# Second product with tokens as weights and w_out moving, leftover tokens of two batches in one sum

## Chip, core and metric

One NeuronCore of one Trainium2 chip runs one program. The metric is the device time of one execution in microseconds (us); the time before is the median of three runs. TensorE (PE) multiplies, VectorE (DVE), ScalarE (ACT) and GpSimd (POOL) do the rest, SyncE (SP) issues the transfers.

## What is computed

```python
a = softmax(phi, axis=seq)                  # [8, 8 heads, 576, 32 slots]
k_m = einsum('bhsm,bhsd->bhmd', a, k)       # d = 64
v_m = einsum('bhsm,bhsd->bhmd', a, v)
attn = softmax(q @ k_m.T / 8)               # [8, 8, 576, 32]
x = (attn @ v_m) as [8 * 576, 512]
h = x @ w_in                                # [4608, 2048]
out = gelu(h) @ w_out                       # [4608, 512]
```

All inputs are float32 but the two weights, which arrive as float64 bits and are converted on the chip (softmax sums carry a small 1e-9, left out here).

## The kernel before

The attention output enters only the first product, so that is taken as attn @ U with U = v_m @ w_in: its contraction runs over 8 heads x 32 slots = 256 rows of one batch (two groups g of 128 partitions) in place of 512. Both large products split their operands into two parts of 12 significant bits (float32r; `_hi` and `_lo`, or `gh` and `gl`) and take high x high, high x low and low x high.

A batch has 576 tokens, worked in two halves of 288. The hidden features come in 16 chunks f of 128. One step is (batch, half, f):

- `hidden` (L544): 6 matmuls with U as weights and the half's attention `p_hi`/`p_lo` moving, 288 wide, into one PSUM tile `h` (two of them in turn).
- `gelu` on ACT (L557) to `gf`, then on DVE the cast `gh` (helper, L126) and the difference `gl` (L563).
- `project` (L580): 12 matmuls, 4 blocks of 128 output features times three products, with w_out (`wo_hi`, `wo_lo`) as weights and `gh`/`gl` moving, 288 wide, into the four sums `acc`. The output therefore comes out transposed, features on the partitions.
- `evict` at a half's end (L598 to L604): DVE and ACT copy the four sums in turn to tiles `o`, four buffers, and SP sends each to `outT`.

`project` follows `hidden` two steps behind (LAG = 2). The first batch is cut in segments of f that alternate between the halves, with partial sums in `part`, while the weights are still being converted (`wi_y`, `wo_y`, `wi_raw`, `wo_raw` and the split `wo_lo`, L158 to L189); its order is a string, START, and every engine takes its part of it as it stands there. Behind it the tile framework's scheduler orders each engine. Around the steps goes a plan: `put(t, ...)` gives each piece of the next batch's attention and of its U a step, and no piece may stand more than AHEAD = 4 steps early.

The attention of a batch: exps of phi (L226, and L282 with tokens on partitions), slot products `pk` (L291), transposes `ptk` (L316), scores `psc` (L350), the softmax on DVE and ACT (exp L385), `p_hi`/`p_lo`. ACT loads a table at each change between exp and gelu. U of batch 1 is made by `absorb` (L482, copies L489/L490); from batch 2 on a pair of batches shares `absorb2`: three matmuls 512 wide (L463), an ACT cast (L467), a DVE difference (L468), and an ACT copy of the second batch's half to `uf` (L469), which `u_split` divides later. U has nine tiles in turn; two make up a block of 512 hidden features. `pk`, `ptk`, `psc` and `pu` all take turns in two PSUM tiles (`at`).

Of the kernel before, what the change touches and what calls it, by code (L numbers as in the profile page):

```python
# [39 lines left out]
gh.6 gl.6 dD.o.6 dD.i.7 dB.o.7 Uh.5 Ul.5 Uh.4 gl.7 dE.6 Lwi.13 p.5 p.6 Ul.4 anorm.1  # L40
# [12 lines left out]
def slot_attention_gelu_ffn(  # L53
    ctx: ExitStack,
    tc: tile.TileContext,
    phiT: bass.AP,  # [B, 2, 128 (4 heads, m), S]
    phiN: bass.AP,  # [B, S, 256 (heads, m)]
    qT: bass.AP,  # [B, 4, 128 (2 heads, d), S]
    kv: bass.AP,  # [B, 2, S, 4 heads, (k | v) 128]
    w_in: bass.AP,  # [512, 2048], float64 bits in int64  # L60
    w_out: bass.AP,  # [2048, 512], float64 bits in int64
    outT: bass.AP,  # [512, B * S]
):
# [25 lines left out]
    W_MAX = 8053061632.0  # the float32 with bits 0x4FEFFFFF  # L89
# [150 lines left out]
    def a_T(b, g, c0):  # L240
        """a of 4 heads with positions on the partitions, from chunk c0 on."""
        aT = tile_of(
            ("aT", b), lambda: sb.tile([P, NC, G, P], F32, tag="aT", name=f"aT_{b}", bufs=1)
        )
        cs = range(c0, min(c0 + 4, NC))
        pool, tag = (ps_acc, f"acc{2 * g + c0 // 4}") if b == 0 else (ps_at, "at")
        pt = pool.tile([P, 4, P], F32, tag=tag, name=f"pt_{b}_{g}_{c0}")
        for n, c in enumerate(cs):
            rows = min(P, S - c * P)
            nc.tensor.transpose(  # L250
                pt[:rows, n, :], st["phi", b][:, g, c * P : c * P + rows], ident
            )
        rows = min(P, S - cs[-1] * P)
        copy("a", aT[:rows, c0 : cs[-1] + 1, g], pt[:rows, : len(cs)])
# [29 lines left out]
    def slots(b, g):  # L284
        """k_m and v_m of 4 heads, [(head, m), (k d | v d)], but the sums of a."""
# [25 lines left out]
    def slots_T(b):  # L311
        """Block-diagonal transposes of k_m and v_m: [(2 heads, d), g, (2 pairs, 2 heads, m)]."""
# [164 lines left out]
    def absorb(b, i, g):  # L477
        """U = v_m @ w_in for 4 heads and 512 of the hidden features, split."""
# [13 lines left out]
    def u0_p(f):  # L492
        """The same for the first batch, all heads and 128 hidden features."""
# [33 lines left out]
    for t, x in enumerate(steps):  # L527
        due.setdefault(x[2], t)
    steps += [
        (b, hf, f, f == 0, f == NF - 1, False)  # L530
        for b in range(1, B)
        for hf in range(2)
        for f in range(NF)
    ]
# [24 lines left out]
    def gelu_hi(t):  # L559
        copy("d", g_tile(t, "gh"), st["gf", t])  # L560

    def gelu_lo(t):
        eng("d").tensor_tensor(  # L563
            g_tile(t, "gl"), st["gf", t], st["gh", t].bitcast(F32), op=ALU.subtract
        )

    def project(t):
        """Adds hidden features f to the half's output."""
# [7 lines left out]
        gh, gl = st["gh", t], st["gl", t]  # L576
# [11 lines left out]
    def evict(t):  # L588
        b, hf, f, first, last, more = steps[t]
        col = b * S + hf * HS  # L590
        for d in range(ND):
# [3 lines left out]
            else:  # L595
                o = sb.tile([P, HS], F32, tag="o", name=f"o_{b}_{hf}_{d}", bufs=4)
# [20 lines left out]
        "h": hidden, "gelu": gelu, "gh": gelu_hi, "gl": gelu_lo, "p": project, "o": evict,  # L617
    }
# [30 lines left out]

    AHEAD = 4  # L650
    n = 2 * NF
    # From batch 2 on, the slots of two batches are made before the first one's U.
    begin = {1: 2, 2: n - 10, 3: n + 3}
    for b in range(1, B):
# [43 lines left out]

    LAG = 2
    for t in range(len(steps) + LAG):  # L700
        if t < len(steps):
            for x in (f"h.{t}", f"gelu.{t}", f"gh.{t}", f"gl.{t}"):
                if x not in done:
                    do(x)
# [3 lines left out]
        if k >= 0:
            if f"p.{k}" not in done:
                do(f"p.{k}")  # L710
            if steps[k][4] and f"o.{k}" not in done:
                do(f"o.{k}")
# [35 lines left out]
```

## Time and profile before

| | us |
|---|---|
| median of 3 runs | 780.12 (779.45 to 780.64) |
| profiled execution, first to last instruction (span) | 777.9 |

The time of a run holds the span and 2.2 us around it, taking the median for the profiled execution's own time. Mean granted TensorE clock: 0.973. A row of a timeline has the start in us, the duration, the engine, the line, the operation and the tiles (out<-in), and in brackets the idle time ahead and what ended it. Rows of groups have the count behind an x, then the summed busy time in us, the mean in ns, and the idle time ahead of them with its releasers. The duration of a matmul is modelled and overlaps the next one; for throughput read the distance of two starts. A window's row has its length, and for each engine the busy time and the count, then the granted clock and the share of the transfers.

### The profile page before, as it was taken

The page shows a single profiled execution, that of the slowest core. Times are in us where ns is not written, and L with a number is a line of the kernel's source. Part 1 is how long each engine was busy: PE and PEld are TensorE (multiplying, and loading weights), DVE is VectorE, ACT ScalarE, POOL GpSimd, SP SyncE. Part 2 cuts the span into 40 slices and gives each one's busy share as a digit, 9 for nine tenths or more (in the row PEclk, how much of TensorE's full clock was granted, in tenths as well). Part 3 has the DMA queues.
Part 4 walks back from the last instruction along what each step waited for, and adds up shares of the span by engine and source line. Part 5 has one row for each costly group of instructions (what it writes and reads, how often), then busy time and mean ns, then how long its engine had stood idle before and what let it go on. Part 6 is the DMA issues. An engine that isn't in the chain of part 4 may idle for free.

```text
span 777.9 us, 14426 instructions
## 1 busy us (share of the span) xinstructions
PE 740.3 (95%) x5772; PEld 693.1 (89%) x5772; DVE 509.9 (66%) x1133; ACT 355.7 (46%) x653; POOL 64.5 (8%) x59
## 2 busy tenths in 40 slices
PE   6487889999999999999999999999999999999998
PEld 4276777879999999999999999999999999999997
DVE  3999999756489645766479655756469654755332
ACT  3757567544256435355146435446147532323211
POOL 1566532100000000000000000000000000000000
PEclk8678999999999999999999999999999999999999
DMA  9856552043220140151220040061120010100000
GB/s 287 300 157 210 170 207 86 4 150 123 62 62 1 40 145 31 35 187 55 62 62 1 31 153 32 5 210 62 62 61 2 31 32 25 39 22 10 14 18 32
DMA packets 44932, 63.72 MB, mean 82 GB/s; under 512 B 3520, under 2 KB 31552, under 8 KB 44864
## 3 DMA queue, kind: packets, MB, share of 16 engines
q1 hardware_dynamic: 44864, 62.80, 25.0%
q8 instruction: 45, 0.74, 0.4%
q14 instruction: 23, 0.19, 0.1%
HBM read 53.35 MB, written 9.44 MB: 81 GB/s over the span
## 4 chain that ended last, share of the span: by engine, by line
PE 87%; DVE 7%; issue 2%; DMA 1%; POOL 1%; ACT 1%; SPq 1%; DVEq 0%; POOLq 0%
PE acc L580 50%; PE h L544 25%; PE pu L463 4%; PE pk L291 3%; PE psc L350 2%; DMA kv<-kv 1%; PE pu L482 1%; DVE gl L563 1%; POOL w_in_sb L176 1%; DVE wo_raw L166 1%; DVE wi_raw L166 1%; DVE wo_y L165 1%; DVE wo_y L169 1%; POOL wo_y L183 1%; PE pu L501 1%
## 5 line engine op out<-in xcount | busy, mean ns | idle before, releaser
L580 PE MATMUL acc<-gh,wo_hi 128*128 128x288 f32 x1024 | 309.1, 302 | 3.8 <-DVE part L602 3.8
L580 PE MATMUL acc<-gl,wo_hi 128*128 128x288 f32 x1024 | 303.4, 296 | 3.1 <-DVE gl L563 2.8
L580 PE MATMUL acc<-gh,wo_lo 128*128 128x288 f32 x1024 | 305.2, 298 | 0.0
L557 ACT ACTIVATE gf<-h 128x288 f32<-128x288 f32 x256 | 104.8, 411 | 306.5 <-PE h L544 259.7
L544 PE MATMUL h<-p_hi,U 128*128 128x288 f32 x1024 | 221.5, 298 | 10.0 <-DVE U L516 7.1
L580 PEld LDWEIGHTS acc<-gh,wo_hi 128*128 128x128 f32 x1024 | 194.3, 190 | 20.6 <-issue 9.3
L126 DVE CAST gh<-gf 128x288 fp32r<-128x288 f32 x250 | 77.7, 311 | 200.8 <-ACT gf L557 200.5
L580 PEld LDWEIGHTS acc<-gl,wo_hi 128*128 128x128 f32 x1024 | 194.6, 190 | 4.3 <-DVE gl L563 3.4
L580 PEld LDWEIGHTS acc<-gh,wo_lo 128*128 128x128 f32 x1024 | 194.8, 190 | 3.1 <-issue 1.0
L544 PEld LDWEIGHTS h<-p_hi,U 128*128 128x128 f32 x1024 | 167.1, 192 | 13.1 <-DVE U L516 8.6
L563 DVE TENSOR_TENSOR gl<-gf,gh 128x288 fp32r<-128x288 f32 x254 | 121.8, 482 | 13.2 <-ACT gh L126 0.3
L544 PE MATMUL h<-p_lo,U 128*128 128x288 f32 x512 | 111.9, 301 | 1.2 <-DVE p_lo L423 1.2
L544 PEld LDWEIGHTS h<-p_lo,U 128*128 128x128 f32 x512 | 83.3, 191 | 1.5 <-DVE p_lo L423 1.5
L469 ACT COPY uf<-pu 64x512 f32<-64x512 f32 x48 | 27.9, 581 | 42.0 <-DVE U L468 41.9
L557 ACT ACT_TABLE_LOAD x31 | 39.8, 1283 | 1.7 <-PE h L544 0.9
L467 ACT CAST U<-pu 64x512 fp32r<-64x512 f32 x48 | 27.9, 582 | 13.2 <-PE pu L463 13.0
L468 DVE TENSOR_TENSOR U<-pu,U 64x512 fp32r<-64x512 f32 x48 | 33.0, 688 | 1.4
L436 DVE TENSOR_TENSOR wl<-w_in_sb,wh 128x512 fp32r<-128x512 f32 x48 | 32.8, 684 | 0.7
L176 POOL TENSOR_TENSOR w_in_sb<-wi_y,wi_raw 128x512 int32<-128x512 int32 x16 | 25.7, 1609 | 46.4 <-DVE wi_y L169 29.4
L291 PE MATMUL pk<-kv,aT 128*32 128x128 f32 (+1 forms) x640 | 24.9, 292 | 3.6 <-DMA kv<-kv 2.6
L291 PEld LDWEIGHTS pk<-kv,aT 128*32 128x32 f32 (+1 forms) x640 | 16.6, 114 | 10.5 <-issue 5.3
L183 POOL TENSOR_TENSOR wo_y<-wo_y,wo_raw 128x512 int32<-128x512 int32 x16 | 23.9, 1492 | 22.7 <-DVE wo_y L169 11.6
(95 smaller groups left out, 645.3 us busy)
## 6 DMA issues: line engine op xcount, KB each, us to landing
kv<-kv SPq DMA_DIRECT2D x64, 256.0 KB, 4.4
q<-qT SPq DMA_DIRECT2D x16, 576.0 KB, 4.1
outT<-o SPq DMA_DIRECT2D x64, 144.0 KB, 1.8
wi_raw<-w_in SPq DMA_DIRECT2D x16, 512.0 KB, 5.7
wo_raw<-w_out SPq DMA_DIRECT2D x16, 512.0 KB, 7.0
phi<-phiT SPq DMA_DIRECT2D x16, 288.0 KB, 4.8
aT<-phiN SPq DMA_DIRECT2D x6, 512.0 KB, 5.5
kv<-kv SPq DMA_DIRECT2D x16, 128.0 KB, 4.6
```

Source lines behind the costliest of these rows:

```text
L126: return e.copy(dst, src) if e is nc.scalar else e.tensor_copy(dst, src)
L176: nc.gpsimd.tensor_tensor(w_in_sb[:, :, f * P : (f + 1) * P].bitcast(I32), y.bitcast(I32).rearrange(parts, c=ND), low.rearrange(parts, c=N ...
L183: nc.gpsimd.tensor_tensor(y.bitcast(I32), y.bitcast(I32), low, op=ALU.add)
L291: nc.tensor.matmul(pk[32 * j : 32 * j + 32, :P], st["aT", b][:rows, c, g, 32 * j : 32 * j + 32], t[:rows, j, :], start=(c == 0), stop=(c = ...
L436: nc.vector.tensor_tensor(w_lo, w, w_hi.bitcast(F32), op=ALU.subtract)
L463: nc.tensor.matmul(pu, v.rearrange("p a n -> p (a n)"), w, start=(k == 0), stop=(k == 2))
L467: nc.scalar.copy(u[own, 0, :], pu[own])
L468: nc.vector.tensor_sub(u[own, 1, :], pu[own], u[own, 0, :].bitcast(F32))
L544: i = nc.tensor.matmul(h[:, :HS], u[g][w], x[:, g, :], start=(n == 0), stop=(n == 3 * G - 1))
L557: nc.scalar.activation(g_tile(t, "gf"), st["h", t][:, :HS], AF.Gelu)
L563: eng("d").tensor_tensor(g_tile(t, "gl"), st["gf", t], st["gh", t].bitcast(F32), op=ALU.subtract)
L580: nc.tensor.matmul(acc[d][:, :HS], w[:, f, ds_], x, start=(first and n == 0), stop=(last and n == 2),)
```

## The change

Batches 1 to 7 (all but the first; counting from 1, from batch 2 on) swap the second product's operands: `gh` and `gl` of 128 tokens are the weights and a row block of w_out, 512 features wide, moves. A batch's 576 tokens are four blocks of 128 and 64 left over. So both halves of a chunk are worked in succession (f is now the outer loop, the half the inner one), the gelus of both fill one tile of 512 columns and a tail of 64, and cast and difference run on 512 columns at once. The 64-column tails of all 16 chunks are kept, and those of two batches (2 and 3, 4 and 5, 6 and 7) go through the second product together behind the odd batch; batch 1 has no partner. The output has tokens on its partitions; the first batch keeps its transposed form (`out0T`).

To have both halves' attention ready at a batch's start, and to make room, other things move: attention of both halves and U are planned at other steps; `o` has two buffers instead of four, `gl` and `kT` two instead of three; `vT` uses the tiles of `uf`; `p_hi`/`p_lo` take three turns, one of which (V) occupies U tiles; two more U tiles hold the tails, so five are left in turn for U. In START one piece moves (gl.7 behind p.5).

```diff
-    for t in range(len(steps) + LAG):  # h, gelu, gh, gl of t; plan; p of t - LAG
...
+    behind = [f"p.{n - 1}", f"o.{n - 1}"]
+    for b in range(1, B):
+        for f in range(NF):
+            t = n * b + 2 * f
+            for hf in range(2):
+                dos(f"H.{b}.{f}.{hf}", f"G.{b}.{f}.{hf}")
+                first[t + hf] = st["hi", b, f, hf]
+                if hf:
+                    dos(f"Gh.{b}.{f}", f"Gl.{b}.{f}")
+                run(t + hf)
+            dos(*behind)
+            behind = [f"P.{b}.{f}"]
+        behind += [f"O.{b}.{j}" for j in range(NT)]
+        if b % 2:
+            for k in range(NFB):
+                dos(f"Tg.{b}.{k}")
+                dos(*behind)
+                behind = [f"T.{b}.{k}"]
+            behind += [f"To.{b}"]
+    dos(*behind)
...
+    def gelu_n(b, f, hf):
+        h, gf = st["h", b, f, hf], g_of("gf", b, f)
+        if hf == 0:
+            nc.scalar.activation(gf[:, :HS], h[:, :HS], AF.Gelu)
+        else:
+            nc.scalar.activation(gf[:, HS:], h[:, : MAIN - HS], AF.Gelu)
+            nc.scalar.activation(tail(b, f)[:, b % 2], h[:, MAIN - HS : HS], AF.Gelu)
...
+    def products(acc, f, gh, gl):
+        for n, (x, w) in enumerate(((gh, wo_hi), (gh, wo_lo), (gl, wo_hi))):
+            nc.tensor.matmul(
+                acc, x, w[:, f, :], start=(f == 0 and n == 0), stop=(f == NF - 1 and n == 2)
+            )
+
+    def project_n(b, f):
...
+        for j in range(NT):
+            js = slice(j * P, (j + 1) * P)
+            products(st["acc", b][j], f, gh[:, js], gl[:, js])
+
+    def tail_project(b, k):
...
+        r = slice(TL * (b % 2), TL * (b % 2) + TL) if alone(b) else slice(0, P)
+        for n in range(4):
+            js = slice(n * P + r.start, n * P + r.stop)
+            products(st["tacc", b][: r.stop - r.start], 4 * k + n, gh[:, js], gl[:, js])
+
+    def evict_n(b, j):
+        o = sb.tile([P, DM], F32, tag="o", name=f"o_{b}_{j}", bufs=NO)
+        copy("da"[j % 2], o, st["acc", b][j])
+        r = b * S + j * P
+        nc.sync.dma_start(out[r : r + P, :], o)
+
+    def tail_evict(b):
+        o = sb.tile([P, DM], F32, tag="o", name=f"to_{b}", bufs=NO)
+        bs = (b,) if alone(b) else (b - 1, b)
+        copy("a", o[: TL * len(bs)], st["tacc", b][: TL * len(bs)])
+        for x, c in enumerate(bs):
+            r = c * S + MAIN
+            nc.sync.dma_start(out[r : r + TL, :], o[TL * x : TL * x + TL])
...
-        attend(b, 0, t + 21)
+        attend(b, 0, t + (17 if b > 1 else 22))
+        put(t + (19 if b > 1 else 23), f"Lq.{b}.1")
+        attend(b, 1, t + 26)
...
-                    put(t + 18 + 4 * i + 4 * g, f"U.{b}.{i}.{g}")
+                    put(t + 26.5 + 8 * i + 2 * g, f"U.{b}.{i}.{g}")
...
-                    put(t + 18 + 4 * i + c - 2, f"W.{b}.{i}.{c}")
-                    put(t + 18 + 4 * i + c, f"U2.{b}.{i}.{c}")
+                    put(t + 20 + 8 * i + 2 * c, f"W.{b}.{i}.{c}")
+                    put(t + 22 + 8 * i + 2 * c, f"U2.{b}.{i}.{c}")
-        put(t + n, f"Lq.{b}.1")
-        attend(b, 1, t + n + 3)
```

**DVE towards the end of the first batch's weights.** Rows in order of DVE's queue, before; the `U` row is the difference that the first product's chunk 11 waits for, the row behind it the second batch's first U.

```order
L126 CAST gh_1177<-gf_1175 128x288
L165 TENSOR_SCALAR wi_y<-wi_y 128x512
L563 TENSOR_TENSOR gl_1179<-gf_1175,gh_1177 128x288
L189 TENSOR_TENSOR wo_lo<-wo_y,wo_hi 128x512
L516 TENSOR_TENSOR U_10_1148<-pu_11_1197,U_10_1148 128x2x128
L490 TENSOR_TENSOR U_0_0_1204<-pu_0_0_1205,U_0_0_1204 128x512
L189 TENSOR_TENSOR wo_lo<-wo_y,wo_hi 128x512
```

The same place of DVE's queue after the change:

```order
L139 CAST gh_1177<-gf_1175 128x288
L182 TENSOR_SCALAR wo_y<-wo_y 128x512
L202 TENSOR_TENSOR wo_lo<-wo_y,wo_hi 128x512
L542 TENSOR_TENSOR U_10_1148<-pu_11_1197,U_10_1148 128x2x128
L589 TENSOR_TENSOR gl_1179<-gf_1175,gh_1177 128x288
L202 TENSOR_TENSOR wo_lo<-wo_y,wo_hi 128x512
L178 TENSOR_SCALAR wi_y<-wi_y 128x512
```

The U difference of chunk 11 now stands ahead of this `gl` and of the step `wi_y`, and the second batch's U (L490) has gone from here; with it, on PE, the product `pu_0_0` (L482) that stood behind `pu_11`.

**ACT in the middle of batch 2, before.** Casts `U` and copies `uf` belong to `absorb2` of a pair; `gf` rows are gelus, the table load and `sT` an exp of the scores.

```order
L467 CAST U_0_1_2522<-pu_0_3_2568 64x512
L469 COPY uf_0_2445<-pu_0_3_2568 64x512
L557 ACTIVATE gf_2598<-h_1_6_2591 128x288
L467 CAST U_1_0_2613<-pu_1_0_2615 64x512
L385 ACT_TABLE_LOAD
L385 ACTIVATE sT_0_2562<-sT_0_2562 128x576
L469 COPY uf_1_2614<-pu_1_0_2615 64x512
L557 ACT_TABLE_LOAD
L557 ACTIVATE gf_2645<-h_1_7_2638 128x288
```

After the change, ACT around chunks 7 to 9 of batch 2:

```order
L493 CAST U_3_0_3045<-pu_3_0_3047 64x512
L659 ACT_TABLE_LOAD
L659 ACTIVATE gf_7_3043<-h_1_7_3058 128x224
L495 COPY uf_3_3046<-pu_3_0_3047 64x512
L660 ACTIVATE tails_1801<-h_1_7_3058 128x64
L657 ACTIVATE gf_8_3090<-h_0_8_3083 128x288
L493 CAST U_3_0_3045<-pu_3_1_3092 64x512
L239 ACT_TABLE_LOAD
L239 ACTIVATE phi_3103,sm_3201<-phi_3103,nm_3183 128x576
L495 COPY uf_3_3046<-pu_3_1_3092 64x512
L659 ACT_TABLE_LOAD
L659 ACTIVATE gf_8_3090<-h_1_8_3106 128x224
```

The exps of phi for the batch after next (L239) now stand among these casts and copies, one just ahead of this piece and one inside it; before they stood in chunks without `absorb2`.

**PE in the same chunk, after the change.** `pu_3_1` stands just ahead of the six matmuls of `h_1_8`, whose last is the first row; then come the scores `psc` of the next batch and chunk 7's second product in its new form.

```order
L647 MATMUL h_1_8_3106<-p_hi_V,U_2_1_2952 128x288
L365 MATMUL psc_0_0_3119<-q_0_2964,kT_2262 64x288 x2
L686 MATMUL acc_0_2790<-wo_hi,gh_7_3067 128x512
L686 MATMUL acc_0_2790<-wo_lo,gh_7_3067 128x512
L686 MATMUL acc_0_2790<-wo_hi,gl_7_3069 128x512
L686 MATMUL acc_1_2791<-wo_hi,gh_7_3067 128x512
L686 MATMUL acc_1_2791<-wo_lo,gh_7_3067 128x512
L686 MATMUL acc_1_2791<-wo_hi,gl_7_3069 128x512
L365 MATMUL psc_0_1_3124<-q_0_2964,kT_2262 64x288 x2
L686 MATMUL acc_2_2792<-wo_hi,gh_7_3067 128x512
```

`psc_0_1` takes the PSUM tile that `pu_3_1` had, which ACT's copy `uf` releases; six matmuls 512 wide stand ahead of it and six behind. Before, each chunk had 12 matmuls of 128x288 here per half, with `wo` as weights.

More of the change, by code (lines that the diff above doesn't have):

```diff
@@ L61, in slot_attention_gelu_ffn @@
     w_out: bass.AP,
-    outT: bass.AP,
+    out0T: bass.AP,
+    out: bass.AP,
 ):
@@ L88, in slot_attention_gelu_ffn @@
     NU = 2 * NFB + 1
+    NO = 2
+    NT = S // P
+    MAIN = NT * P
+    TL = S - MAIN
     W_MAX = 8053061632.0
@@ L98, in slot_attention_gelu_ffn @@
     ones = const.tile([P, P], F32, name="ones")
+    ident = const.tile([P, P], F32, name="ident")
+    parity = const.tile([P, 96], F32, name="parity")
+    w_in_sb = const.tile([P, ND, DFF], F32, name="w_in_sb")
+    wo_hi = const.tile([P, NF, DM], F32R, name="wo_hi")
+    wo_lo = const.tile([P, NF, DM], F32R, name="wo_lo")
     nc.vector.memset(ones, 1.0)
@@ L322, in slots_T @@
         if b < 2:
-            vT = st["vT", b] = sb.tile([P, G, P], F32, tag="vT", name=f"vT_{b}")
+            vT = st["vT", b] = sb.tile(
+                [P, G, P], F32, tag="uf", name=f"vT_{b}"
+            )
             copy("a", vT, v)
@@ L412, in p_tile, with make @@
     def p_tile(w, b, hf):
+        k = 2 * b + hf
+        turn = k if k < 2 else 2 - (k - 2) % 3
+        if turn == 2:
+            def make():
+                t = sb.tile([P, 4 * DM // 2], F32R, tag="U", name=f"{w}_V", bufs=NU)
+                return t[:, : G * HS].rearrange("p (g s) -> p g s", g=G)
+            return tile_of((w, "V"), make)
         return tile_of(
-            (w, b, hf), lambda: sb.tile([P, G, HS], F32R, tag=w, name=f"{w}_{b}_{hf}")
+            (w, b, hf),
+            lambda: sb.tile([P, G, HS], F32R, tag=f"{w}{turn}", name=f"{w}_{b}_{hf}", bufs=1),
         )
@@ L425, in p_lo @@
             st["pT", b, hf][:, g],
-            st["p_hi", b, hf][:, g].bitcast(F32),
+            p_tile("p_hi", b, hf)[:, g].bitcast(F32),
             op=ALU.subtract,
@@ L528, in slot_attention_gelu_ffn @@
         due.setdefault(x[2], t)
[L529 to L534, printed above, removed]
     def hidden(t):
@@ L603, in evict, with tail, hidden_n @@
             if f == NF - 1:
-                nc.sync.dma_start(outT[d * P : (d + 1) * P, col : col + HS], o)
+                nc.sync.dma_start(out0T[d * P : (d + 1) * P, hf * HS : (hf + 1) * HS], o)
+    def tail(b, f):
+        t = tile_of(
+            ("tails", f // 8),
+            lambda: sb.tile([P, 8, 2, TL], F32, tag="U", name=f"tails_{f}", bufs=NU),
+        )
+        return t[:, f % 8]
+    def hidden_n(b, f, hf):
+        u = [st["U", b, f, g] for g in range(G)]
+        ph, pl = p_tile("p_hi", b, hf), p_tile("p_lo", b, hf)
+        h = st["h", b, f, hf] = ps_h.tile([P, FB], F32, tag="h", name=f"h_{b}_{hf}_{f}")
+        n = 0
+        for w, x in ((0, ph), (0, pl), (1, ph)):
+            for g in range(G):
+                i = nc.tensor.matmul(
+                    h[:, :HS], u[g][w], x[:, g, :], start=(n == 0), stop=(n == 3 * G - 1)
+                )
+                if n == 0:
+                    st["hi", b, f, hf] = i.ins.name
+                n += 1
@@ new lines, in gelu_n, with hi_n, lo_n @@
+    def gelu_n(b, f, hf):
[5 more added lines that the diff above has]
+            nc.scalar.activation(tail(b, f)[:, b % 2], h[:, MAIN - HS : HS], AF.Gelu)
+    def hi_n(b, f):
+        copy("d", g_of("gh", b, f), g_of("gf", b, f))
+    def lo_n(b, f):
+        nc.vector.tensor_tensor(
+            g_of("gl", b, f), g_of("gf", b, f), g_of("gh", b, f).bitcast(F32), op=ALU.subtract
+        )
@@ new lines, in alone, with tail_split @@
+    def alone(b):
+        return b == 1
+    def tail_split(b, k):
+        x = st["tails", k // 2][:, k % 2 * 4 : k % 2 * 4 + 4]
+        gh, gl = (
+            g_of(w, "t", b, k).rearrange("p (f x n) -> p f x n", f=4, x=2) for w in ("gh", "gl")
+        )
+        if alone(b):
+            x, gh, gl = (y[:, :, b % 2] for y in (x, gh, gl))
+        nc.vector.tensor_copy(gh, x)
+        nc.vector.tensor_tensor(gl, x, gh.bitcast(F32), op=ALU.subtract)
+    def products(acc, f, gh, gl):
+        for n, (x, w) in enumerate(((gh, wo_hi), (gh, wo_lo), (gl, wo_hi))):
+            nc.tensor.matmul(
+                acc, x, w[:, f, :], start=(f == 0 and n == 0), stop=(f == NF - 1 and n == 2)
+            )
@@ new lines, in project_n @@
+    def project_n(b, f):
+        if f == 0:
+            st["acc", b] = [
+                ps_acc.tile([P, DM], F32, tag=f"acc{j}", name=f"acc_{b}_{j}") for j in range(NT)
+            ]
+        gh, gl = g_of("gh", b, f), g_of("gl", b, f)
+        for j in range(NT):
+            js = slice(j * P, (j + 1) * P)
+            products(st["acc", b][j], f, gh[:, js], gl[:, js])
+    def tail_project(b, k):
+        if k == 0:
+            st["tacc", b] = ps_acc.tile([P, DM], F32, tag="acc0", name=f"tacc_{b}")
+        gh, gl = (g_of(w, "t", b, k) for w in ("gh", "gl"))
+        r = slice(TL * (b % 2), TL * (b % 2) + TL) if alone(b) else slice(0, P)
+        for n in range(4):
+            js = slice(n * P + r.start, n * P + r.stop)
+            products(st["tacc", b][: r.stop - r.start], 4 * k + n, gh[:, js], gl[:, js])
@@ L697, in run, with dos @@
                     tc.add_manual_dep(i, first[t - AHEAD], edge, reason="step")
+    def dos(*xs):
+        for x in xs:
+            if x not in done:
+                do(x)
     LAG = 2
-    for t in range(len(steps) + LAG):
[L701 to L704, printed above, removed]
+    for t in range(n + LAG):
+        if t < n:
+            dos(f"h.{t}", f"gelu.{t}", f"gh.{t}", f"gl.{t}")
             first[t] = st["hi", t]
-        run(t)
+            run(t)
         k = t - LAG
[L708 to L712, printed above, removed]
+        if k >= 0 and k < n - 1:
+            dos(f"p.{k}", *([f"o.{k}"] if steps[k][4] else []))
+    behind = [f"p.{n - 1}", f"o.{n - 1}"]
[18 more added lines that the diff above has]
+    dos(*behind)
     last = {}
@@ L742 @@
     ]
-    outT = nc.dram_tensor("outT", (moe_w_out.shape[1], B * S), F32, kind="ExternalOutput").ap()
+    DM = moe_w_out.shape[1]
+    out0T = nc.dram_tensor("out0T", (DM, S), F32, kind="ExternalOutput").ap()
+    out = nc.dram_tensor("out", (B * S, DM), F32, kind="ExternalOutput").ap()
     with tile.TileContext(nc) as tc:
-        slot_attention_gelu_ffn(tc, *args, outT)
+        slot_attention_gelu_ffn(tc, *args, out0T, out)
     r = run_bass_kernel_spmd(nc, [arrays], core_ids=[0])
-    return np.ascontiguousarray(r.results[0]["outT"].T)
+    return np.concatenate([r.results[0]["out0T"].T, r.results[0]["out"][S:]])
```

35 lines of the change are left out of this document (18 added, 17 removed).

## Prediction

> **What bounds the kernel now.** I read the page first: the busy shares, the slices of the span and the chain that ended last.
>
> ```profile
> PE 740.3 (95%) x5772; PEld 693.1 (89%) x5772; DVE 509.9 (66%) x1133; ACT 355.7 (46%) x653; POOL 64.5 (8%) x59
> PE   6487889999999999999999999999999999999998
> PE 87%; DVE 7%; issue 2%; DMA 1%; POOL 1%; ACT 1%; SPq 1%; DVEq 0%; POOLq 0%
> PE acc L580 50%; PE h L544 25%; PE pu L463 4%; PE pk L291 3%; PE psc L350 2%; DMA kv<-kv 1%; PE pu L482 1%; DVE gl L563 1%; POOL w_in_sb L176 1%; DVE wo_raw L166 1%; DVE wi_raw L166 1%; DVE wo_y L165 1%; DVE wo_y L169 1%; POOL wo_y L183 1%; PE pu L501 1%
> ```
>
> TensorE (PE) is busy 95% of the span, and from the seventh slice to the last but one it is full. Half of the chain is the second product (L580), a quarter the first (L544). A mean over the whole span hides where the others matter, so next came the windows:
>
> ```profile
> core 0: us, PE busy (x) PEld busy (x) DVE busy (x) ACT busy (x) POOL busy (x), PEclk, DMA share, GB/s
> 100.00:120.00 20.00, 16.25 (x149) 13.07 (x148) 19.93 (x38) 11.08 (x25) 7.22 (x5) 1.00 0.48 163
> 200.00:400.00 200.00, 200.00 (x1636) 190.90 (x1635) 125.32 (x294) 89.90 (x163) 0.00 (x0) 1.00 0.22 69
> 702.56:773.95 71.39, 71.39 (x542) 71.39 (x540) 28.10 (x71) 16.65 (x35) 0.00 (x0) 1.00 0.03 9
> ```
>
> There are two regimes. Up to about 120 us VectorE (DVE) is full (19.93 of 20) and PE waits for it; behind that PE is full at a granted clock of 1.00. So in seven batches out of eight the time is the sum of the PE's starts, and a wait of PE that the change makes is paid in full. A faster DVE or ACT is worth nothing there.
>
> **The second product: the price of one matmul.** A matmul's own duration overlaps the next one's, so what counts is the step from start to start. For 288 columns the window from 702.56 to 773.95 has nothing but 30 steps of 6 + 12 matmuls: 71.39 us / 540 = 132.2 ns. For 512 columns the kernel has one place, the three matmuls of L463, 48 times. First and last of the 48:
>
> ```profile
> 215.87 0.39 PE L463 MATMUL pu<-wh,v_hi 128*128 128x512 f32 x1
> ...
> 216.57 0.30 PE L580 MATMUL acc<-gh,wo_hi 128*128 128x288 f32 x1
> 617.11 0.39 PE L463 MATMUL pu<-wh,v_hi 128*128 128x512 f32 x1
> ...
> 617.82 0.30 PE L580 MATMUL acc<-gh,wo_hi 128*128 128x288 f32 x1
> ```
>
> Three take 0.70 and 0.71 us; over the 48 the mean is 698.8 ns, the least 686, the most 702. That is 232.9 ns for one, between 228.7 and 234. Then 512/288 = 1.78 times the columns cost 1.76 times the time: nearly all of the price is columns, and only about 3 ns are a fixed cost that fewer matmuls could save.
>
> The change takes away, in batches 1 to 7, 7 x 2 x 16 x 12 = 2688 matmuls of 288 and puts in 7 x 16 x 12 = 1344 of 512 for the whole blocks of 128 tokens and 4 x 48 = 192 for the leftovers (three pairs, and batch 1 alone, which pays full columns for half of the tokens): 1536. The columns go from 774,144 to 786,432. Before 2688 x 132.2 = 355.4 us, after 1536 x 232.9 = 357.8 us: **+2.4 us**, with the bounds of the triples -4.2 to +4.0.
>
> The weights need a look of their own, since each matmul loads new ones:
>
> ```profile
> L463 PEld LDWEIGHTS pu<-wh,v_hi 128*128 128x128 f32 x48 | 9.0, 188 | 0.0
> L580 PEld LDWEIGHTS acc<-gh,wo_lo 128*128 128x128 f32 x1024 | 194.8, 190 | 3.1 <-issue 1.0
> ```
>
> A load of 128x128 takes 188 to 190 ns at either width, longer than the 132.2 ns step, so loads already overlap each other and are not a floor; at 232.9 ns they are hidden with more to spare. [...]
>
> **What the other engines get.** Per hidden chunk DVE had two casts and two subtractions:
>
> ```profile
> L563 DVE TENSOR_TENSOR gl<-gf,gh 128x288 fp32r<-128x288 f32 x254 | 121.8, 482 | 13.2 <-ACT gh L126 0.3
> L126 DVE CAST gh<-gf 128x288 fp32r<-128x288 f32 x250 | 77.7, 311 | 200.8 <-ACT gf L557 200.5
> L126 DVE CAST wh<-w_in_sb 128x512 fp32r<-128x512 f32 x48 | 20.1, 419 | 0.3
> L436 DVE TENSOR_TENSOR wl<-w_in_sb,wh 128x512 fp32r<-128x512 f32 x48 | 32.8, 684 | 0.7
> ```
>
> 2 x (311 + 482) = 1586 ns become one cast and one subtraction of 512 columns, 0.42 + 0.684 = 1.1 us, and about 0.14 as a share of the tails. DVE loses some 0.35 us of each 4.4 us that PE needs for a chunk (12 x 0.132 + 12 x 0.233). PE was full, so this relief buys nothing. ACT gets one gelu instruction more per chunk, well inside its 46%. The copies of the sums go from 288 to 512 columns and stand beside the next chunk's matmuls. These I cost at nothing; the cover is PE's full queue.
>
> **The start.** The change takes the second batch's first U product (L482) out of the stretch in which PE waits for DVE:
>
> ```profile
> 114.22 1.03 PE L482 MATMUL pu<-w_in_sb,vT 128*64 128x512 f32 x4
> 115.18 0.40 PE L580 MATMUL acc<-gh,wo_hi 128*128 128x288 f32 x1
> 119.32 0.54 PE L544 MATMUL h<-p_hi,U 128*128 128x288 f32 x2 [1.54 <-DVE U L516]
> ```
>
> The product took 0.96 us there, and behind it PE waited 1.54 us for DVE's U all the same; it was free, and in the full stretch it costs 0.96. On DVE the work ahead of that U also changes:
>
> ```profile
> 101.88 0.41 DVE L165 TENSOR_SCALAR wi_y<-wi_y 128x512 f32<-128x512 f32 x1
> ...
> 116.44 1.53 DVE L165 TENSOR_SCALAR wi_y<-wi_y 128x512 f32<-128x512 f32 x1
> 117.88 0.45 DVE L563 TENSOR_TENSOR gl<-gf,gh 128x288 fp32r<-128x288 f32 x1
> 118.25 0.68 DVE L189 TENSOR_TENSOR wo_lo<-wo_y,wo_hi 128x512 fp32r<-128x512 f32 x1
> 118.85 0.41 DVE L516 TENSOR_TENSOR U<-pu,U 128x256 fp32r<-128x256 f32 x1
> ```
>
> In the new order the decode step wi_y and this gl stand behind the U. The gl is 0.37 from start to start, and wi_y took 1.44, most of it a hold-up that would as well strike the instruction in its place; at 101.88 the same form takes 0.41. So the U is done about 0.7 us earlier: 0.96 - 0.7 = **+0.3 us**. Bounds: +0.96 if the wait ends when it did, and -0.6 if the whole 1.54 us go.
>
> **The border of batch 0.** The output copies of batch 0 had four buffers and now have two. The third copy must wait until the first one's transfer has landed.
>
> ```profile
> L598 DVE TENSOR_TENSOR o<-acc,part 128x288 f32<-128x288 f32 x8 | 3.3, 453 | 0.6 <-PE acc L580 0.6
> outT<-o SPq DMA_DIRECT2D x64, 144.0 KB, 1.8
> ```
>
> 0.45 + 1.8 + 0.45 = 2.7 us after the last product of that half the third sum is free. The new order has 19 matmuls of 288 before the first one that writes there, 19 x 132.2 = 2.5 us. That leaves 0.2, and as much again as the fourth copy may be late: I take **+0.3**, bounds 0 and 2 (a whole landing, if DVE comes to the first copy late). Between later batches stand 12 matmuls of the first product and six of 512, 1.6 + 1.4 = 3.0 us, against 0.6 + 1.8 + 0.6 = 3.0 with copies of 512 columns: even, so nothing is counted, and the tails' matmuls stand there as well after odd batches.
>
> **ACT's queue in batches 2 and 4.** U of a pair of batches is made block by block ahead of its use, one ACT cast and one ACT copy to each 0.70 us triple; the copy releases the PSUM buffer. New is that the exps of the next slots (phi) fall into the same chunks, each with a table load ahead and another behind it.
>
> ```profile
> L557 ACT ACT_TABLE_LOAD x31 | 39.8, 1283 | 1.7 <-PE h L544 0.9 <-issue 0.2
> L467 ACT CAST U<-pu 64x512 fp32r<-64x512 f32 x48 | 27.9, 582 | 13.2 <-PE pu L463 13.0
> L469 ACT COPY uf<-pu 64x512 f32<-64x512 f32 x48 | 27.9, 581 | 42.0 <-DVE U L468 41.9
> L226 ACT ACTIVATE phi<-phi,nm 128x576 f32<-128x576 f32 x16 | 12.4, 775 | 4.1 <-DVE nm L220 4.0
> ```
>
> ```profile
> 701.44 1.19 PE L350 MATMUL psc<-q,kT 128*64 128x288 f32 x8
> 702.56 0.40 PE L580 MATMUL acc<-gh,wo_hi 128*128 128x288 f32 x1
> 702.80 0.30 PE L580 MATMUL acc<-gh,wo_lo 128*128 128x288 f32 x1
> ```
>
> In chunk 8 ACT runs cast, table load, exp, copy: 0.58 + 1.28 + 0.78 + 0.58 = 3.2 us from the triple to the release. PE wants that buffer for psc_0_1 after six matmuls of 288, two of psc (eight took 1.12 up to the next start, so 0.28, and 0.11 for the change of kind: the step behind it is 0.24 where the next is 0.14) and six of 512: 0.8 + 0.4 + 1.4 = 2.6 us. It waits 0.6, or 0.75 with the hand-over, and this stands in the middle of a project step, so everything is behind it. Twice: **+1.5 us**, bounds 0 (the exps' loads in time and the copy ahead) and 3 (ACT already late by one cast and a gelu).
>
> **Small change.** Four more changes between kinds of matmul stand in the order; one costs 0.11, as above: **+0.4**, bounds 0 and 0.5. At the end the last copy has 512 columns and two transfers instead of one:
>
> ```profile
> 774.28 0.40 ACT L600 COPY o<-acc 128x288 f32<-128x288 f32 x1 [0.39 <-PE acc L580]
> ```
>
> 0.58 (L469, the same number of columns) for 0.40, and the second transfer issued after the first: I take **+0.6**, bounds 0.2 (the copy alone) and 2 (one landing of 1.8 behind the other).
>
> **Sum.** 2.4 + 0.3 + 0.3 + 1.5 + 0.4 + 0.6 = +5.5 us. The profiled execution has a span of 777.9; the median of the runs is 780.12, so 2.2 us lie around the span. 777.9 + 2.2 + 5.5 = **785.6 us**. All low bounds together would give 775.5, all high ones 792.6; they don't fall together.
>
> **Rivals.**
>
> *Faster: the wide stream runs better in a long row than in triples.* If the step of the 1344 + 192 falls to what a weight load needs, 190 ns, the second product costs 291.8 us, the change gains 63.6 there and the time is about 720. A mild form, in which a triple carries some 30 ns of entering and leaving, makes it 223 ns, 342.5 us, -12.9: about 770. It decides from a step under 228.3 ns on, where the stream's gain (4.7 us) outweighs the other terms' 3.1 by 1.6. For it: the weight loads are busy in all of the 71.39 us of that window, and the change takes away 1152 of their 2688 in the second product. Against: the least triple of 48 is 228.7, and steps before, inside and behind a triple are all what their columns make them. [...] Chance 0.09, most of it for the mild form.
>
> *No change: the stream as in the shorter triples, and no waits.* At 230 ns (690 ns for three) the second product costs 353.3, -2.1; ACT's copies come in time, and DVE's earlier U gives back the moved product. With the end and the changes of kind, +1.0, the sum is -1.1, and with one of the waits +0.5: 779.0 to 780.6, or 781.6 with the mean triple. For it: ACT is only half busy, and the order is no clock. Against: the mean triple. Chance 0.15.
>
> *Slower by much: U's tiles come too late.* Nine tiles become five, so while the block in use and the next one hold four, only one tile is free; the second group's cast waits until PE has finished a block, and behind that cast in ACT's queue stands the gelu that PE's next product needs. If the cast stands a chunk too early, PE loses what is left of a gelu's slack at each of the 12 blocks of the three pairs, some 0.4 us (one gelu, 0.41) each: +5, and 791. Planned slack is two half steps, 4.4 us, against it. Chance 0.12.
>
> *The forecast*, 782 to 789: chance 0.64.
>
> **How the numbers follow.** Some 0.2%, 1.6 us, is what a measurement here can tell from no change. Faster than 778.6 is the first rival, 0.09; within 778.6 to 781.7 the second, 0.15; slower the rest, 0.76. For 8 in 10 the range leaves out the first rival, the lower half of the second and the upper half of the third: **780.2 to 790.5**.
>
> **What would show it.** Right: steps of about 233 ns in the new L686 rows, between 230 and 235 everywhere; one DVE wait ahead of the U of chunk 11 that is shorter than 1.54; a PE wait of 0.5 to 1.0 us at psc_0_1 (L365) in batches 2 and 4 that ACT's copy (L495) ends; and PE full elsewhere. Wrong: a step of the new rows under 228 ns (then the stream was mispriced), new waits on ACT gelus or U casts, or a PE wait in the rows of the tails.

## The result, and the profile after

| | before | after |
|---|---|---|
| median of 4 runs each, us | 780.38 (779.45 to 781.02) | 788.10 (787.65 to 789.23) |
| ratio, 95% interval | | 1.0105 (1.0088 to 1.0121) |
| profiled span, us | 777.9 | 786.4 |

The changed kernel is slower by 7.7 us where 5.5 were forecast; 788.1 lies in the range of 780.2 to 790.5. The sum was near in part by luck: the step of the wide stream came as worked out, one forecast wait did not exist, and the largest loss lies in a place that the prediction had priced at 0.6 us. The busy shares, slices and chain of the page of after:

```profile
PE 744.4 (95%) x4620; PEld 621.2 (79%) x4620; DVE 487.5 (62%) x927; ACT 365.7 (46%) x759; POOL 65.4 (8%) x59
PE   6477888999999999999999999999999999999997
PE 81%; DMA 1%; DVE 0%; POOL 0%; issue 0%; SPq 0%; ACT 0%; POOLq 0%; DVEq 0%
PE acc L686 40%; PE h L647 23%; PE tacc L686 6%; PE pu L489 4%; PE psc L365 2%; PE pk L304 2%; PE acc L606 2%; PE pu L508 1%; PE h L564 1%; DMA kv<-kv 1%; PE pn L290 0%; PE ptk L329 0%; POOL w_in_sb L189 0%; SPq L221 0%; PE pu L527 0%
```

TensorE is the bound as before, with 1152 fewer matmuls and 4 us more of busy time; the weight loads fell from 89% to 79% of the span and VectorE from 66% to 62%, and the time did not fall with them. The windows of after, with the columns of those of before:

```profile
200.00:400.00 200.00, 199.79 (x1236) 163.61 (x1229) 120.00 (x232) 92.92 (x193) 0.00 (x0) 1.00 0.22 68
700.00:760.00 60.00, 60.00 (x331) 52.42 (x330) 20.99 (x38) 12.90 (x43) 0.00 (x0) 1.00 0.05 18
```

In the batches proper TensorE is as full as it was. **The new waits stand ahead of them**, while the first batch ends. TensorE's timeline of after from chunk 11's U product (112.76) to 150 us, the rows that began with an idle time, and the first with a slow step behind the last of them:

```profile
116.54 0.40 PE L564 MATMUL h<-p_hi,U 128*128 128x288 f32 x1 [0.67 <-DVE U L542]
...
126.07 0.40 PE L606 MATMUL acc<-gh,wo_hi 128*128 128x288 f32 x1 [0.71 <-DVE part L623]
...
129.28 0.40 PE L564 MATMUL h<-p_hi,U 128*128 128x288 f32 x1 [1.35 <-ACT gf L583]
...
143.03 0.66 PE L527 MATMUL pu<-w_in_sb,vT 128*64 128x128 f32 x8 [1.64 <-POOL w_in_sb L189]
143.62 0.47 PE L606 MATMUL acc<-gh,wo_lo 128*128 128x288 f32 x1
143.89 0.44 PE L606 MATMUL acc<-gl,wo_hi 128*128 128x288 f32 x1
```

These are 4.37 us of waits against the one of 1.54 at the same place before. (The wait for chunk 10's U just ahead, 1.23 where it was 0.73, is in neither.) The step of the last two rows is 0.27 us where 288 columns took 0.13; the windows say why (the column ahead of the last two is the granted clock):

```profile
140.39:143.81 3.42, 1.78 (x16) 1.32 (x16) 1.79 (x5) 0.22 (x2) 3.42 (x2) 1.00 0.00 0
143.81:147.22 3.41, 3.41 (x16) 2.38 (x15) 2.35 (x5) 1.89 (x4) 0.42 (x1) 0.50 0.02 5
147.22:150.63 3.41, 3.41 (x24) 2.35 (x20) 3.28 (x8) 0.41 (x1) 0.00 (x0) 1.00 0.00 0
```

TensorE counts as busy behind the wait, but for 3.41 us at half its clock: 0.50 x 3.41 = 1.7 us are lost. The window of 3.42 us ahead of that stretch was idle for 1.64, while the 1.54 us before the change and the 1.35 above left the clock at 1.00.

A ledger says how much that makes. It adds up TensorE's steps, each from a matmul's start to the next one's, from chunk 11's U product (113.74 before, 112.76 after) to the last matmul (773.95 and 781.62), us:

| | before | after | two U products early (below) |
|---|---|---|---|
| second product | 386.1 | 389.0 (+2.9) | 388.1 (+2.0) |
| first product | 193.1 | 196.5 (+3.4) | 193.1 (0.0) |
| scores psc | 15.8 | 17.7 (+1.8) | 16.1 (+0.3) |
| U, slots, transposes | 65.1 | 65.7 (+0.6) | 66.5 (+1.4) |
| sum | 660.2 | 668.9 (+8.7) | 663.9 (+3.7) |

A wait counts in the row of the matmul ahead of it, so the waits and the slow clock sit in the first three rows, the second product's too. Split at the first batch's last matmul (at about 168 us), its +2.9 is +1.9 ahead of the split and +1.0 behind it, and the first product's +3.4 is +1.5 and +1.9; with two U products early these are +1.0 and +1.0, -1.8 and +1.8. The 1.9 of the first product behind the split come mostly from its steps that lead to a matmul of U, slots or transposes: 73 of 161 ns, before 67 of 146.

From the last matmul's start to the end the span has 3.97 us before and 4.82 after. (The stretch ahead of chunk 11 does not come out the same in each execution: in the profiled one of after it ended 1.0 us earlier than before, and in the seventh experiment, whose order is the same there, 2.0 later.)

### The profile page after: what moved, and what is told of

It is laid out like the page before. It is cut to its first block, busy times and chain, and to the rows that moved or that the text cites. A ratio compares the mean times of both kernels' runs of the same rounds, so it can differ in the third digit from the quotient of the medians.

```text
span 786.4 us, 11903 instructions
## 1 busy us (share of the span) xinstructions
PE 744.4 (95%) x4620; PEld 621.2 (79%) x4620; DVE 487.5 (62%) x927; ACT 365.7 (46%) x759; POOL 65.4 (8%) x59
## 4 chain that ended last, share of the span: by engine, by line
PE 81%; DMA 1%; DVE 0%; POOL 0%; issue 0%; SPq 0%; ACT 0%; POOLq 0%; DVEq 0%
PE acc L686 40%; PE h L647 23%; PE tacc L686 6%; PE pu L489 4%; PE psc L365 2%; PE pk L304 2%; PE acc L606 2%; PE pu L508 1%; PE h L564 1%; DMA kv<-kv 1%; PE pn L290 0%; PE ptk L329 0%; POOL w_in_sb L189 0%; SPq L221 0%; PE pu L527 0%
## 5 line engine op out<-in xcount | busy, mean ns | idle before, releaser
L686 PE MATMUL acc<-wo_hi,gh 128*128 128x512 f32 x448 | 179.1, 400 | 0.0
L686 PE MATMUL acc<-wo_lo,gh 128*128 128x512 f32 x448 | 177.0, 395 | 0.0
L686 PE MATMUL acc<-wo_hi,gl 128*128 128x512 f32 x448 | 176.8, 395 | 0.0
L686 PEld LDWEIGHTS acc<-wo_hi,gh 128*128 128x128 f32 x448 | 84.2, 188 | 23.2 <-issue 4.9
L686 PEld LDWEIGHTS acc<-wo_hi,gl 128*128 128x128 f32 x448 | 84.1, 188 | 21.0 <-issue 0.4
L686 PEld LDWEIGHTS acc<-wo_lo,gh 128*128 128x128 f32 x448 | 84.2, 188 | 15.1
L666 DVE TENSOR_TENSOR gl<-gf,gh 128x512 fp32r<-128x512 f32 x112 | 76.6, 684 | 4.7
L606 PE MATMUL acc<-gh,wo_hi 128*128 128x288 f32 x128 | 41.7, 327 | 6.8 <-DVE part L627 6.1
L606 PE MATMUL acc<-gl,wo_hi 128*128 128x288 f32 x128 | 40.4, 316 | 3.0 <-DVE gl L589 2.7
L606 PE MATMUL acc<-gh,wo_lo 128*128 128x288 f32 x128 | 40.1, 314 | 0.0
```

What stands on the lines that cost most here:

```text
L606: nc.tensor.matmul(acc[d][:, :HS], w[:, f, ds_], x, start=(first and n == 0), stop=(last and n == 2),)
L666: nc.vector.tensor_tensor(g_of("gl", b, f), g_of("gf", b, f), g_of("gh", b, f).bitcast(F32), op=ALU.subtract)
L686: nc.tensor.matmul(acc, x, w[:, f, :], start=(f == 0 and n == 0), stop=(f == NF - 1 and n == 2))
```

## The experiments

Theory: **cover**. Until chunk 15's weights are converted, the first batch goes at the pace of ACT, DVE and POOL. Before, three of batch 1's eight U products stood ahead of chunk 15's U product and two more just behind it, and kept TensorE at work; the change plans all eight later, so TensorE arrives early and waits, and must still do them when it is full. (The expectation of the fourth run counts all five as standing ahead; the order shows three.) Rivals: the converted chunk 15 comes late by itself; ACT and DVE are what is full there; or the loss belongs to the new form or to the smaller buffers.

**1. Two U products early.**

```diff
-                    put(t + 26.5 + 8 * i + 2 * g, f"U.{b}.{i}.{g}")
+                    put(t + (18 + 4 * g if i < 1 else 26.5 + 8 * i + 2 * g), f"U.{b}.{i}.{g}")
```

> The changed kernel with one edit: batch 1's first two U products (block 0) are planned where the kernel before had them, at steps t+18 and t+22, so they stand ahead of chunk 15's U product on TensorE. Cover theory: up to that product the first batch is paced by the conversion of the weights, TensorE idles there, and the U products that the change moved out of this stretch were free; two products of 0.96 us come back under cover, so 788.1 - 1.9 = 786.2, and down to 784.4 if the 1.64 us wait for the converted chunk 15 and the slowed clock behind it go too. Rival (VectorE and ScalarE are what is full there, so U's cast and difference cost as much as they save): 788 or more, with new waits on VectorE. Rival (the loss sits in the wide second product): 788.

Measured: 783.49 (782.39 to 786.76, 9 runs), ratio to before 1.0039 (1.0024 to 1.0053), against 1.0105 for the change. Two products that take 1.9 us won 4.6, and the time is 0.9 below the lowest that was expected. (The profiled execution is the slowest of the nine, 786.76; chunk 11's U product starts in it at 116.25 us, 2.5 later than before.) All the waits that its timeline has left up to 150 us behind the one for chunk 10:

```profile
125.80 0.40 PE L606 MATMUL acc<-gl,wo_hi 128*128 128x288 f32 x1 [0.19 <-DVE gl L589]
130.18 1.08 PE L508 MATMUL pu<-w_in_sb,vT 128*64 128x512 f32 x4 [0.53 <-DVE sT L378]
```

The waits of 1.35 and 1.64 are gone. Its windows:

```profile
132.00:140.00 8.00, 8.00 (x63) 6.83 (x64) 6.59 (x19) 6.25 (x10) 0.00 (x0) 1.00 0.46 167
140.00:148.00 8.00, 8.00 (x66) 6.69 (x63) 6.55 (x16) 4.35 (x10) 2.63 (x2) 1.00 0.01 2
```

TensorE is full and the clock stays at 1.00. Up to the ledger's split the same matmuls take 5.2 us less than in after, behind it 0.2 more: the whole gain lies in the first batch's end.

**2. Chunk 15 converted early.**

```diff
-    for f, t in ((12, 11.5), (11, 17.25), (13, 20.75), (14, 21.5), (15, 24.25)):
+    for f, t in ((12, 11.5), (11, 17.25), (13, 20.75), (14, 21.5), (15, 22.5)):
```

> The changed kernel with one edit: chunk 15's weights are loaded and converted from step 22.5 instead of 24.25. If TensorE's 1.64 us wait for the converted chunk and the half clock in the 3.5 us behind it (some 1.8 us) are a loss of their own, both go and the time is 784.7 (784 to 785.5). Rival (the conversion, VectorE and ScalarE queues are full, another wait takes its place): 787.5 to 788.5, with a wait on VectorE or ScalarE of about the same length a few us later.

Measured: 788.24 (787.73 to 790.41), the rival's number, though the rival looked for the new wait a few us later and not earlier. TensorE's wait for chunk 15 is gone, and these have come or grown:

```profile
127.55 0.40 PE L606 MATMUL acc<-gh,wo_hi 128*128 128x288 f32 x1 [1.46 <-DVE part L623]
135.50 0.53 PE L564 MATMUL h<-p_hi,U 128*128 128x288 f32 x2 [1.86 <-DVE U L542]
```

The wait at 143.03 was where TensorE's lead over the others came out, and not its cause: with that one removed, the lead comes out 7.5 us earlier.

**3. Both edits.**

> Both edits, the two U products and chunk 15's conversion early. Cover theory: 783 (782 to 784.5): the wait, the slowed clock and 1.9 us of U products go. Rival (queues full): not below e1 and e2, 786 or more.

Measured: 787.18 (784.65 to 788.28), ratio 1.0078 (1.0053 to 1.0104): no gain on the first experiment but a loss, in the rival's range. Its trace has one long wait of TensorE, for a cast of DVE:

```profile
143.85 0.40 PE L606 MATMUL acc<-gh,wo_hi 128*128 128x288 f32 x1 [1.78 <-DVE gh L139]
```

DVE's rows ahead of that cast in the same run:

```profile
139.41 1.80 DVE L179 SCALAR_TENSOR_TENSOR wo_raw<-wo_raw 128x512 int32<-128x512 int32 x1
141.13 0.41 DVE L182 TENSOR_SCALAR wo_y<-wo_y 128x512 int32<-128x512 int32 x1
141.47 0.25 DVE L411 RECIPROCAL smx<-smx 128x18 f32<-128x18 f32 x1
141.75 1.82 DVE L416 TENSOR_TENSOR sT<-sT,smx 128x576 f32<-128x576 f32 x1
143.50 0.30 DVE L139 CAST gh<-gf 128x288 fp32r<-128x288 f32 x1
```

My expectation was wrong: chunk 15's conversion now stands ahead of the step's own cast, and two of DVE's instructions there took 1.8 us, of forms that take 0.68 and 0.77 in the mean of after. GpSimd worked at both times:

```profile
139.24 1.41 POOL L189 TENSOR_TENSOR w_in_sb<-wi_y,wi_raw 128x512 int32<-128x512 int32 x1 [11.27 <-DVE wi_y L182]
141.68 1.28 POOL L196 TENSOR_TENSOR wo_y<-wo_y,wo_raw 128x512 int32<-128x512 int32 x1 [1.02 <-ACT U L139]
```

In the traces of before and after, each of the 66 DVE instructions (34 and 32) that took over 0.4 us more than the fastest of the same line, tiles and shape overlapped an instruction of GpSimd, and of the 1846 that overlapped none, none took more than 0.1 us above it. So in these traces the hold-up goes with GpSimd's work; no run tried these conversions without it.

**4. The kernel before, with its U products late.** Nothing of the second product is changed.

```diff
-                    put(t + 18 + 4 * i + 4 * g, f"U.{b}.{i}.{g}")
+                    put(t + 26.5 + 4 * i + 2 * g, f"U.{b}.{i}.{g}")
```

> The kernel before with one edit: batch 1's U products are planned from step t+26.5 on, as the change has it (but every two steps, since its halves come one after the other), so all five that stood ahead of chunk 15's U product now stand behind it; nothing of the second product is changed. Cover theory: five products of 0.96 us lose their cover, the time goes from 780.4 to between 783 and 785.2. Rival (the loss comes from the new form, from two gl or o buffers or from both halves' attention standing ahead of batch 1): 780.4 unchanged, within 0.5.

Measured: 784.56 (782.5 to 786.53, 6 runs), ratio 1.0053 (1.0035 to 1.0071). This is the deciding run: an edit of the plan alone costs the old kernel 4.5 us. The waits of its timeline behind chunk 11's U product (the profiled execution is the fastest of the six, 782.5):

```profile
115.79 0.53 PE L544 MATMUL h<-p_hi,U 128*128 128x288 f32 x2 [0.82 <-ACT U L126]
118.11 0.53 PE L544 MATMUL h<-p_hi,U 128*128 128x288 f32 x2 [1.26 <-DVE U L516]
128.92 0.53 PE L544 MATMUL h<-p_hi,U 128*128 128x288 f32 x2 [0.19 <-ACT gf L557]
133.97 0.54 PE L544 MATMUL h<-p_hi,U 128*128 128x288 f32 x2 [0.42 <-ACT U L126]
141.33 0.43 PE L501 MATMUL pu<-w_in_sb,vT 128*64 128x128 f32 x2 [0.78 <-POOL w_in_sb L176]
```

They add up to 3.47 us, against the one of 1.54 in the kernel before. So neither the new form nor the smaller buffers are needed for a loss of that size.

**5. Four U products early** (blocks 0 and 1, the second at steps t+24 and t+25).

> As the run with two U products early, but with four of batch 1's U products (blocks 0 and 1) ahead of chunk 15's U product. There TensorE already had no wait left but 0.72 us behind 116 us, so if cover is what counts nothing is left to win: 783.5 (783 to 784.5). Rival (each U product that stands early saves its 0.96 us): 781.6.

Measured: 785.64 (785.0 to 787.51), ratio 1.0067 (1.0047 to 1.0087). The rival's 781.6 is out: once TensorE is full, further products there are work like any other. That it is 2 us slower than with two was not expected. Its trace has two waits that the run with two hasn't, 1.5 us together; what brought them was not tried:

```profile
145.55 0.66 PE L527 MATMUL pu<-w_in_sb,vT 128*64 128x128 f32 x8 [0.65 <-POOL w_in_sb L189]
149.13 0.71 PE L365 MATMUL psc<-q,kT 128*64 128x288 f32 x4 [0.87 <-DVE U L542]
```

**6. Batch 1's leftovers with w_out as weights** and 64 columns moving, two U products early.

```diff
+        if alone(b):
...
+                for d in range(ND):
+                    ds_ = slice(d * P, (d + 1) * P)
+                    for m, (w, x) in enumerate(((wo_hi, gh), (wo_lo, gh), (wo_hi, gl))):
+                        nc.tensor.matmul(
+                            st["tacc", b][d], w[:, f, ds_], x[:, js],
...
```

> Two U products early, and batch 1's 64 leftover tokens taken as before the change, with w_out as weights and 64 columns moving: 192 matmuls 128x64 in place of 48 of 64x512. By the price by column (0.455 ns a column and 3 ns, 32 ns each) they cost 6.1 us in place of 11.2, 778.4 in all and less than the kernel before. By the weight loads as a floor of narrow matmuls (a load takes 188 ns and loads go in at least every 132 ns in the 288-wide stream) they cost 25 us: 797. In between a load's floor of 60 to 100 ns: 784 to 792. The step between two of the new matmuls tells which.

Measured: 810.56 (808.57 to 812.09), ratio 1.0382 (1.0354 to 1.0410), slower than any of the cases. The narrow matmuls of its timeline, at two places:

```profile
258.70 0.28 PE L714 MATMUL tacc<-gl_t,wo_hi 128*128 128x64 f32 x1
258.81 0.29 PE L714 MATMUL tacc<-gh_t,wo_hi 128*128 128x64 f32 x1
258.93 0.39 PE L714 MATMUL tacc<-gh_t,wo_lo 128*128 128x64 f32 x1
259.13 0.40 PE L714 MATMUL tacc<-gl_t,wo_hi 128*128 128x64 f32 x1
259.34 0.40 PE L714 MATMUL tacc<-gh_t,wo_hi 128*128 128x64 f32 x1
```

The step is 0.11 us and then 0.21, and its windows show the granted clock fall while TensorE and its weight loads are busy without a gap:

```profile
253.00:256.00 3.00, 3.00 (x30) 3.00 (x29) 1.19 (x3) 0.58 (x1) 0.00 (x0) 1.00 0.51 193
259.00:262.00 3.00, 3.00 (x16) 3.00 (x15) 0.00 (x0) 0.00 (x0) 0.00 (x0) 0.50 0.01 3
270.00:278.00 8.00, 8.00 (x39) 8.00 (x39) 0.00 (x0) 0.00 (x0) 0.00 (x0) 0.50 0.00 0
283.00:286.00 3.00, 3.00 (x29) 3.00 (x29) 0.95 (x2) 0.38 (x1) 0.00 (x0) 1.00 0.00 0
```

At the full clock a matmul with a new 128x128 of weights thus takes 0.11 us at 64 columns, some 80 ns more than the 32 by the price of its columns. The 288-wide step of 0.132 lies above that, which fits that the weight loads were busy all the time there (71.39 of 71.39 us) and yet set nothing.

**7. The shared sum undone**: every batch's leftovers alone.

```diff
     def alone(b):
-        return b == 1
+        return True
...
-        if b % 2:
+        if True:
```

> The changed kernel with the shared sum undone: every batch from 1 on takes its 64 leftover tokens through the second product alone, 7 x 48 matmuls of 64x512 in place of 4 x 48. Price by moving columns: 144 more at 0.233 us, +33.6, 821.7 (820 to 823.5). Rival (half the weights' columns, half the price): 788.1 - 5.6 + 16.8 = about 799 to 805.

Measured: 823.13 in one run, 35.0 more than the change, where 33.6 were expected for 144 matmuls. Half as many columns of weights are no cheaper: with 64 of them 11 steps of the last leftovers take 2.55 us, 0.232 each. The moving 512 are what is paid. Its first batch shows the same loss as the change, in another execution:

```profile
146.05 0.66 PE L527 MATMUL pu<-w_in_sb,vT 128*64 128x128 f32 x8 [1.66 <-POOL w_in_sb L189]
```

with a granted clock of 0.74 and 0.50 in the two windows of 2 us behind it.

**8. A quarter of batch 1's leftovers**, two U products early. The kernel leaves out the last 12 of the 16 hidden chunks, 36 of 48 matmuls, in the second product of batch 1's 64 leftover tokens, so these rows are not the reference's.

> Two U products early, and of the second product of batch 1's 64 leftover tokens only the first four of the 16 hidden chunks are done (36 of 48 matmuls left out, so these 64 rows are not the reference's). If TensorE is full there, 36 x 0.233 = 8.4 us less: 775.1 (774 to 776.5). Rival (these matmuls stand beside a wait that is there anyway, the two o buffers or the copies of batch 1's sums): 780 or more.

Measured: 775.71 in one run, 7.8 less than the first experiment, which has the whole of them (8.4 expected). TensorE is full there; batch 1's 64 lone tokens cost 48 x 0.233 = 11.2 us, twice what they would in a pair.

No version that computes the whole result was found to beat the kernel before.

## Why the prediction came out as it did

**The bound and the second product** were right. The last rows of the timeline of after are wide matmuls in a long row:

```profile
779.99 0.39 PE L686 MATMUL tacc<-wo_lo,gh_t 128*128 128x512 f32 x1
...
781.62 0.40 PE L686 MATMUL tacc<-wo_hi,gl_t 128*128 128x512 f32 x1
```

Seven steps take 1.63 us, 232.9 ns each, the triples' mean to the digit, and the mean over all 1535 steps of the new rows is 234.7 with the changes of kind and waits in it. So a triple carries no cost of entering and leaving, and the first rival is out. Behind the ledger's split the second product costs +1.0 where +2.4 was forecast: its 1535 steps after have a mean of 234.7 ns in place of 232.9, and its 2687 steps before, which the change took away, one of 133.7 in place of 132.2. The second rival, 230 ns a step and no waits, is out on both counts. The relief of DVE, priced at nothing, brought nothing that shows.

**The start** (+0.3) **and the border** (+0.3) are the term that was mis-sized: some 4.5 us went there. The step that failed is "the product took 0.96 us there, ... it was free": I looked for cover only where TensorE already waited, found one of the products, and let DVE's earlier U pay for most of it. The others stood where TensorE was full, and I did not see that it was full because of them. With three gone from ahead of chunk 15's (3 x 0.96 = 2.9 us) the waits grow from 1.54 to 4.37 us, by 2.8; the slow clock behind the last of them adds 1.7. The wait for chunk 11's U did get shorter (0.67 for 1.54), but the prediction's own sum does not say so: with the product gone from ahead of it and U 0.7 earlier, the wait would be 1.54 + 0.96 - 0.7 = 1.8, and with the whole wait gone the bound would be 0.96 - 2.5 = -1.5 and not -0.6. U came 1.8 us earlier (its wait ends 3.78 us behind the start of chunk 11's product, before 5.58): the hold-up that struck `wi_y` ahead of it now strikes the `gl` behind it (1.21 us from 116.40). The border itself, the copies waiting for a transfer, cost nothing: no wait of TensorE for an output copy stands in the trace of after behind 143 us.

**ACT's queue in batches 2 and 4** (+1.5) was wrong, and not in size. ACT ran as forecast, but the scores did not wait for it. Chunk 8 of batch 2 in after, rows of TensorE, ACT and DVE:

```profile
309.22 0.40 PE L686 MATMUL acc<-wo_hi,gl 128*128 128x512 f32 x1
309.54 0.71 PE L365 MATMUL psc<-q,kT 128*64 128x288 f32 x4
```

```profile
309.39 0.58 ACT L495 COPY uf<-pu 64x512 f32<-64x512 f32 x1
```

```profile
308.67 0.48 DVE L378 STREAM_TRANSPOSE sT<-psc 128x288 f32<-128x288 f32 x1
```

`psc_0_1` starts at 309.54, before ACT's copy of `pu_3_1` has even ended (309.97), and with no more than the step for a change of kind. The semaphore that it waits on is DVE's. It cannot have taken that tile, as I had it both in the prediction and ahead of it. What ended in time is DVE's transposition of `psc_0_0` (309.15), in whose tile it evidently stands. I gave out the two PSUM tiles by turns, in the order of TensorE's queue. The numbers in the names (`pu_3_1` 3092, `psc_0_0` 3119, `psc_0_1` 3124) rise in that same order, so turns in the order in which the code asks would have been as wrong; what the framework went by is not shown. The cover was short besides: a piece of scores takes 0.64 us to the next start, four rows in the timeline, where the prediction counted two of eight, 0.39. Behind 150 us the trace of after has one wait of TensorE, 0.21 us for `kv`, so batch 4 had none for the scores either.

**The end** (+0.6) is +0.85 by the two spans. **Changes of kind** (+0.4) were priced too low: the first product's steps behind the split alone are +1.9. **U's tiles** never made TensorE wait in the batches proper; the third rival is out.

So misses of both signs left the forecast 2.2 short of the measured 7.7: 1.5 too much for ACT's queue and 1.4 for the second product, some 4 too little for the start and some 1.5 for changes of kind. That they came so near to each other is luck. Experiments 1 and 4 show the start's loss; the rest is read from the ledger and was not tried by itself.

## What to carry to other kernels

Where an engine is full, ask what it would wait for if part of its work were planned elsewhere: work that fills the time until another engine delivers is free only there, and moving it costs it twice, as a wait now and as work later. Before a stream is made wider, measure the step at both widths: here 512 columns cost what 288 cost per column, and by an estimate from the 0.11 us at 64 columns and the price of a column the weight loads would have been a reason only below some 240 columns. Before a wait for a buffer is priced, look up in a trace which release its taker waited for; turns in the order of a queue are a guess.

## What the runs showed of the hardware

TensorE's clock fell to half in two ways that the share of busy time does not show. It went by windows: in the traces of before and after every stretch at one clock, but the one that the trace's end cuts off, is a whole number of 3.41 us. Up to 160 us 11 of their windows at the full clock were followed by one at 0.50; TensorE was idle in them for 1.64 to 3.41 us. The other 57 were idle for at most 1.52, what the wait of 1.54 before the change has in one window, and were followed by one at 1.00. In the seventh experiment the clock fell behind a wait of 1.66 us. Longer ones in the second and third, 1.86 and 1.78 us, left it at 1.00. The 1.86 lay across the end of a window; where the 1.78 lay is not shown. In the second experiment TensorE waited from 133.64 to 135.50:

```profile
131.71:135.13 3.42, 1.93 (x15) 1.69 (x13) 3.42 (x6) 0.74 (x4) 1.99 (x2) 1.00 0.00 0
135.13:138.54 3.41, 3.04 (x25) 2.70 (x26) 3.41 (x8) 2.72 (x5) 0.00 (x0) 1.00 0.00 0
```

So the length of a wait does not decide alone; how much of it lies in one window, 1.49 and 0.37 us here, fits the windows of before and after at the full clock, in which nothing between 1.52 and 1.64 us occurred. And in the sixth experiment the clock fell with no idle time at all, some 6 us into a row of 64-column matmuls with a new weight load each, and stayed at 0.50 for more than 19 us (259 to 278), with TensorE and its weight loads busy in all of it. So being busy with weight loads and narrow matmuls did not keep the clock at 1.00 there; why is not shown.

VectorE's slow instructions stood beside GpSimd's: 34 in the trace of before and 32 in that of after, all of which overlapped one of GpSimd (third experiment). Not each overlap came with one: in either trace 107 of VectorE's instructions overlapped one of GpSimd.
